# A chunked linear recurrence and a feed-forward layer on one core: static stages against a list-scheduled, token-major kernel

## The chip, the cores and the metric

The kernel runs on one core of a Trainium2 chip. The metric is device microseconds of one execution, on the slowest core, which here is the only one. A run is called slow when it lies more than 1.5% above the fastest run of the same kernel on the same chip. Only fast runs enter a ratio.

Engine names follow the profile. PE does matmuls, PEld its weight loads, DVE is the vector engine, ACT the scalar engine, POOL is GpSimd, and SP issues loads.

## The reference

Four batches of eight heads with 768 tokens of 48 values go through a recurrence with a decaying state. The eight heads of a token are then joined to 384 values, which go through 384 → 2048 → 384 with a leaky ReLU.

```python
state = zeros(B, H, D, D)
for t in range(S):                               # S = 768, D = 48
    cur = u * k[t] (outer) v[t]
    y[:, :, t] = r[t] @ (state + cur)
    state = w * state + k[t] (outer) v[t]        # w per head and channel
x = y.transpose(0, 2, 1, 3).reshape(B * S, H * D)      # 3072 x 384
h = x @ w_in                                     # 384 x 2048
out = max(0.01 * h, h) @ w_out                   # 2048 x 384
```

Both kernels cut the recurrence into chunks of 128 tokens, six a batch, so there are 24 stages. Inside a chunk it is a masked product of scores with v, plus the state times a decayed r.

## The kernel before

Each head is padded from 48 to 64 columns, so the 384 values of a token become 512 and fill four slabs of 128 rows. The first layer therefore costs four matmuls for each block of 128 hidden columns. Order is fixed by hand: a stage has four insertion points, and each takes a set number of feed-forward matmuls.

```python
NSLAB = 4
MOE_INSERT = [5, 5, 9, 9]          # feed-forward matmuls allowed at each point of a stage
# ...
# POOL, at the start: seven stages of r, k and v (cast to bf16), then all the weights
for n in range(NRAW):
    issue_input_stage(n)
for dst_ap, src_ap in win_chunks:  sem_w1.inc(g.dma_start(dst_ap, src_ap), 16)
for dst_ap, src_ap in wout_chunks: sem_w2.inc(g.dma_start(dst_ap, src_ap), 16)
# ...
# DVE, one stage: leaky ReLUs of the stage before, preparation of stage n + 4, state
for n in range(NSTAGE):
    for (T, fb) in lrelu_slot[n]:
        lrelu(T, fb)               # scalar_tensor_tensor 128x512: max(0.01 * h, h)
    prep_part1(n + 4)              # k*u, r*(k*u)
    state_update(n)                # waits for the stage's output matmuls
    prep_part2a(n + 4)             # reduce; r*qdec; v*s
    prep_part2b(n + 4)             # k*kdec; k*kbar
# ...
# ACT: first-layer eviction, the input of lrelu
sem_evac.inc(ACT.activation(h_sb[j % NHB][:, :], bank[:, :], AF.Copy))
# SP: one DMA transpose of 128x2048 a stage.  PE: scores, output and state products a stage
```

## Time and profile before

| | before |
|---|---|
| time, median | 276.89 us |
| PE / DVE / ACT / POOL busy | 70% / 67% / 42% / 43% |
| PE busy in the first 80 us | 24.0 us |
| PE busy from 80 to 200 us | 96.9 of 120 us |
| PE busy from 200 us to the end | 73.2 of 76.4 us |

The shares of the span hide three different stages, so the next view cuts the span. First come the page's rows in 40 slices of 6.9 us; a digit is the busy share in tenths, and PEclk is the granted PE clock in tenths.

```profile
PE 194.1 (70%) x1487; PEld 107.6 (39%) x1504; DVE 185.7 (67%) x323; ACT 115.6 (42%) x202; POOL 117.6 (43%) x150
...
PE   0002340126959249779896789997999999999995
...
DVE  5089991060997998789979899998881691186000
...
POOL 8999998064151834616564627741051100000000
PEclk9999999999997757999999999997999999999999
```

The same by windows. Columns after the stretch: its length, then busy us (and instructions) of PE, PEld, DVE, ACT and POOL, then the granted clock, the DMA share and GB/s.

```profile
0.00:80.00 80.00, 24.01 (x210) 14.91 (x212) 46.08 (x93) 21.95 (x35) 57.23 (x78) 1.00 1.83 136
80.00:120.00 40.00, 25.63 (x195) 13.23 (x199) 35.00 (x58) 17.59 (x31) 16.74 (x21) 0.79 1.21 102
120.00:160.00 40.00, 33.48 (x279) 18.08 (x280) 36.75 (x61) 20.28 (x38) 20.63 (x25) 1.00 1.25 116
160.00:200.00 40.00, 37.80 (x314) 21.05 (x316) 36.79 (x65) 22.19 (x40) 16.43 (x19) 0.96 0.91 111
200.00:240.00 40.00, 39.79 (x312) 22.18 (x314) 20.01 (x34) 20.22 (x38) 6.57 (x8) 1.00 0.21 56
240.00:276.40 36.40, 33.42 (x186) 18.11 (x185) 11.08 (x16) 13.33 (x24) 0.00 (x0) 1.00 0.14 50
```

PE is nearly idle at first, then shares the time with a DVE that is 87 to 92% busy, then runs alone.

The chain of waits (start us, length us, what) shows how the middle is tied together. This is one stage of it:

```profile
143.38 0.43 DVE tmp_st L387
...
143.83 0.69 DVE LS L391
...
144.56 0.69 DVE s_tok L346
...
145.60 1.11 DVE QVK L355
146.72 0.77 DVE QVK L363
147.49 0.77 DVE KB L369
148.26 0.61 DVE gT L404
...
148.95 0.60 ACT h_sb L476
...
149.61 0.61 PE ps_moe L535 x2
```

PE waits for an eviction (L476), the eviction for a leaky ReLU to free its buffer (L404), and the leaky ReLU stands in DVE's fixed order behind a whole stage's preparation. The DVE products beside POOL's mask are long: the view of the kdec product's line gives min/median/max in ns.

```profile
L363 DVE TENSOR_TENSOR QVK<-raw,kdec x24: 412/633/864, 16.3 to 205.7; 128x512 bf16<-128x512 bf16 x24
```

### The profile page before, as it was taken

The numbers are of one execution on the slowest core, as the hardware profiler recorded it, in microseconds if no ns is written. First come the engines' busy times: TensorE is split into PE (matmuls) and PEld (weight loads), VectorE is DVE, ScalarE is ACT, GpSimd is POOL, SyncE is SP. The second block draws the span as 40 slices with busy tenths as digits, with TensorE's granted clock in tenths as the row PEclk, the third lists the DMA queues.
The fourth block names the chain that finished last, engine by engine and source line by source line (L and its number), as shares of the span: only waits on it lengthen the run. The fifth ranks groups of instructions, "written<-read, shape, count | busy, mean of one in ns | idle before, by whom it ended". The sixth has DMA issues, their size and how long they took to land.

```text
span 276.4 us, 4070 instructions
## 1 busy us (share of the span) xinstructions
PE 194.1 (70%) x1487; PEld 107.6 (39%) x1504; DVE 185.7 (67%) x323; ACT 115.6 (42%) x202; POOL 117.6 (43%) x150
## 2 busy tenths in 40 slices
PE   0002340126959249779896789997999999999995
PEld 0001230113424134346552356543565446545663
DVE  5089991060997998789979899998881691186000
ACT  1451220013536224473464464565545772365121
POOL 8999998064151834616564627741051100000000
PEclk9999999999997757999999999997999999999999
DMA  3999999999993999849999749994235000200212
GB/s 29 96 129 171 157 105 181 170 151 149 143 152 69 127 70 147 52 80 121 139 160 175 41 82 171 144 157 78 45 90 134 1 2 30 85 2 0 85 59 85
DMA packets 132100, 28.09 MB, mean 102 GB/s; under 512 B 126528, under 2 KB 131648, under 8 KB 132080
## 3 DMA queue, kind: packets, MB, share of 16 engines
q0 software_dynamic: 78704, 10.53, 70.4%
q1 hardware_dynamic: 49920, 12.59, 30.8%
q10 hardware_dynamic: 3456, 4.72, 4.9%
q8 instruction: 12, 0.20, 0.3%
q14 instruction: 8, 0.07, 0.1%
HBM read 20.84 MB, written 4.72 MB: 92 GB/s over the span
## 4 chain that ended last, share of the span: by engine, by line
PE 49%; DVE 21%; POOL 14%; DMA 10%; issue 3%; ACT 2%; ACTq 0%; POOLq 0%
PE ps_moe L540 20%; PE ps_moe L535 20%; DMA raw<-in_v_dram 10%; POOL raw L279 7%; DVE gT L404 6%; DVE QVK L355 3%; DVE LS L391 2%; DVE s_tok L346 2%; DVE QVK L363 2%; POOL raw L275 2%; PE ps_ytr L595 2%; POOL w_out_sb L301 2%; DVE KB L369 2%; PE ps_at L555 2%; PE ps_sinc L576 2%
## 5 line engine op out<-in xcount | busy, mean ns | idle before, releaser
L535 PE MATMUL ps_moe<-xT,w_in_sb 128*128 128x512 bf16 x367 | 93.1, 399 | 16.9 <-ACT h_sb L476 14.0
L476 ACT ACTIVATE h_sb<-ps_moe 128x512 bf16<-128x512 f32 x96 | 57.0, 597 | 50.4 <-DVE gT L404 31.2
L404 DVE SCALAR_TENSOR_TENSOR gT<-h_sb 128x512 bf16<-128x512 bf16 x96 | 63.2, 711 | 14.2 <-ACT h_sb L476 14.0
L540 PE MATMUL ps_moe<-w_out_sb,gT 128*128 128x384 bf16 x384 | 66.6, 326 | 0.0
L535 PEld LDWEIGHTS ps_moe<-xT,w_in_sb 128*128 128x128 bf16 x384 | 37.0, 102 | 58.8 <-ACT h_sb L476 15.7
L463 ACT ACTIVATE ATf<-ps_at 128x512 bf16<-128x512 f32 x48 | 27.7, 596 | 60.8 <-PE ps_at L555 46.1
L279 POOL DMA_DIRECT2D raw<-in_r_dram x24 | 21.7, 906 | 72.5 <-PE ps_ytr L597 70.9
L288 POOL TENSOR_SCALAR_AFFINE_SELECT ATm<-ATf 128x512 bf16<-128x512 bf16 x44 | 34.6, 810 | 30.2 <-ACT ATf L463 30.2
L540 PEld LDWEIGHTS ps_moe<-w_out_sb,gT 128*128 128x128 bf16 x384 | 36.4, 98 | 23.2
L555 PE MATMUL ps_at<-TP 128*128 128x128 bf16 x96 | 11.0, 246 | 47.5 <-DMA TP<-QVK 46.5
L387 DVE TENSOR_TENSOR tmp_st<-LS,WLT 64x512 bf16<-64x512 bf16 x20 | 9.1, 454 | 30.2 <-PE ps_ytr L597 29.9
L555 PEld LDWEIGHTS ps_at<-TP 128*128 128x128 bf16 x96 | 6.4, 107 | 49.4 <-issue 24.0
L481 ACT ACTIVATE out_sb<-ps_moe 128x384 f32<-128x384 f32 x24 | 11.8, 492 | 32.7 <-PE ps_moe L540 32.4
L279 POOL DMA_DIRECT2D raw<-in_v_dram x24 | 21.8, 910 | 0.0
L279 POOL DMA_DIRECT2D raw<-in_k_dram x24 | 21.6, 900 | 0.0
L336 DVE TENSOR_TENSOR ku_buf<-raw,u_tab 128x512 bf16<-128x512 bf16 x24 | 11.4, 476 | 15.0 <-DMA raw<-in_v_dram 15.0
L355 DVE TENSOR_TENSOR QVK<-raw,s_tok 128x512 bf16<-128x512 bf16 x24 | 20.3, 845 | 0.0
L595 PE MATMUL ps_ytr<-ATm,raw 128*64 128x128 bf16 x192 | 16.1, 244 | 3.4 <-DVE ATm L377 2.0
L576 PE MATMUL ps_sinc<-raw,KB 128*64 128x64 bf16 x160 | 9.9, 212 | 11.6 <-DVE LS L391 11.6
L346 DVE TENSOR_REDUCE s_tok<-tmp_buf 128x8 f32<-128x512 bf16 x24 | 16.5, 686 | 0.8
L454 ACT ACTIVATE xT<-ps_ytr 128x512 bf16<-128x512 f32 x24 | 14.4, 600 | 4.9 <-PE ps_ytr L597 4.4
L595 PEld LDWEIGHTS ps_ytr<-ATm,raw 128*64 128x64 bf16 x192 | 11.3, 120 | 11.7 <-issue 9.0
(49 smaller groups left out, 159.7 us busy)
## 6 DMA issues: line engine op xcount, KB each, us to landing
out_dram<-out_sb ACTq DMA_DIRECT2D x24, 192.0 KB, 1.9
raw<-in_r_dram POOLq DMA_DIRECT2D x24, 96.0 KB, 5.2
raw<-in_k_dram POOLq DMA_DIRECT2D x24, 96.0 KB, 5.4
raw<-in_v_dram POOLq DMA_DIRECT2D x24, 96.0 KB, 6.2
w_in_sb<-in_moe_w_in_dram POOLq DMA_DIRECT2D x8, 192.0 KB, 11.8
w_out_sb<-in_moe_w_out_dram POOLq DMA_DIRECT2D x8, 192.0 KB, 18.5
TP<-QVK SPq DMA_TRANSPOSE x24, 5.6
lnw_bc<-in_w_dram POOLq DMA_DIRECT2D x1, 192.0 KB, 4.8
```

Of the source, the lines that this page charges most:

```text
L279: sem_in[bi].inc(g.dma_start(raw[bi][:, xi, :, 0:D], srcap), 16)
L288: inst = g.affine_select(ATm[pi][:, 4 * q:4 * q + 4, :], ATf[q][:, :, :], pattern=[[0, 4], [1, 128]], compare_op=ALU.is_ge, fill=0.0, base ...
L346: sc.inc(V.tensor_reduce(s_tok[pi][:, :], tmp_buf[pi][:, :, :], AX.X, ALU.add))
L355: iv = V.tensor_tensor(QVK[bi][:, :, 0:E], raw[ri][:, 2, :, :], s_tok[pi][:, :].unsqueeze(2).to_broadcast([128, H, E]), ALU.mult)
L404: inst = V.scalar_tensor_tensor(gT[T % 2][:, fb, :], h_sb[j % NHB][:, :], LRELU_SLOPE, h_sb[j % NHB][:, :], ALU.mult, ALU.max)
L463: sem_atev.inc(ACT.activation(ATf[q][:, :, :], ps_at[q][:, :].rearrange("p (m i) -> p m i", i=128), AF.Copy))
L476: sem_evac.inc(ACT.activation(h_sb[j % NHB][:, :], bank[:, :], AF.Copy))
L535: inst = PE.matmul(bank[:, :], w_in_sb[:, m, 128 * gd["x"]:128 * gd["x"] + 128], xT[:, m, 512 * gd["T"]:512 * gd["T"] + 512], start=first, ...
L540: inst = PE.matmul(bank[:, 0:DM], gT[gd["T"] % 2][:, s, 128 * gd["x"]:128 * gd["x"] + 128], w_out_sb[:, s, :], start=first, stop=lastm)
L555: last = PE.matmul(ps_at[0][:, 128 * hh:128 * hh + 128], TP[bi1][:, 2 * hh + 1, :], TP[bi1][:, 2 * hh, :])
L576: last = PE.matmul(ps_sinc[64:128, 64 * hh:64 * hh + 64], KB[bi1][:, hh, :], raw[ri1][:, 2, hh, :])
L595: PE.matmul(ps_ytr[pi][prow, pcol], raw[ri][:, 2, hh, :], ATm[pi][:, hh, :], start=True, stop=False)
```

## The change

The kernel is written anew. It builds a list of operations with estimated durations, reads, writes and buffer pools, and a list scheduler orders every engine's instructions and derives the semaphores. The intent is to keep PE full. The work itself changes too:

- x is dense (three slabs instead of four), because the recurrence's output is token-major and PE transposes it.
- The decay is centred, so that tables serve 256 tokens. The state stays in PSUM over two chunks.
- Loads go uncast from SP's queue. The u-bonus moves to POOL, and the score mask to DVE, read from PSUM.
- The first eight stages are transposed on PE, and later ones by DMA, at half the size.
- The leaky ReLU is an eviction, a scaled copy (by ACT or by DVE) and one wide maximum on DVE over 2048 columns.
- Feed-forward groups of one stage (the first two), then of two, are interleaved with the recurrence from the first stage on; the kernel before groups four stages. Filler matmuls are meant to keep PE's clock up at the start.

```diff
-NSLAB = 4
-MOE_INSERT = [5, 5, 9, 9]
+GROUPS = [1, 1] + [2] * 11
+TWO = [1, 1, 1, 1] + [1, 1, 0, 0] * 4 + [0, 0, 0, 0]
+QKT_DMA_FROM = 8
+WARM_UNTIL = 14.0
+DMA_SEQ = "st0 wc st1 u wi0@rk0 wi1@rk0 st2@v1 wo0@rk2 st3@v2 wo1@v2 st4@rk3"
 # ... the scheduler: among the ready operations of an engine the earliest start, then priority
+                    key = (max(st, free[e] + 0.02), o.prio)
+                    if best is None or key < best[0]:
+                        best = (key, o, st, sl)
 # ... loads: 0.14 and 0.07 us of SP time are planned, 2.1 and 1.05 us of transfer
+        o1 = op("SP", 0.14, go_rk, f"ldrk{n}", prio, writes=[vr], xfer=2.1, ndma=2, after=after)
+        o2 = op("SP", 0.07, go_v, f"ldv{n}", prio + 0.01, writes=[vrv], behind=[o1], xfer=1.05)
 # ... weights: 0.48 us of transfer are planned for a block of 128 hidden columns
+                  writes=[f_wi[i]], after=after, xfer=0.48 * WI[i], sem=f"wi{i}")
 # ... one stage of the recurrence
+        o = op("DVE", 0.96, lambda: V.tensor_tensor(kq.t[:, :, 0:D], ..., tab[l]..., ALU.mult), ...)
+            op(bn, bd_, lambda: be.tensor_tensor(pu.t[:, :, :], vr.t[:, 1, :, :], ubc[:, :, :], ALU.mult), ...)   # POOL
+            op(bn, bd_, lambda: be.tensor_tensor(pr.t[:, :, :], pu.t[:, :, :], vr.t[:, 0, :, :], ALU.mult), ...)  # POOL
+            op("DVE", 1.23, lambda: V.tensor_tensor(at.t[:, :, :], xy..., tri..., ALU.mult), ...)
+        op("DVE", 0.57, lambda: V.tensor_tensor(ys.t[:, :], y.t[:, 0:DM], bv.t[:, :], ALU.add), ...)
 # ... first layer of T stages: three slabs
+                    for s in range(3):
+                        o = PE.matmul(bk.t[:, 128 * T * f:128 * T * (f + 1)], win[:, s, 128 * fb:128 * fb + 128],
+                                      xT[:, s, L * n0:L * n0 + L * T], start=(s == 0), stop=(s == 2))
+            e1 = op("ACT", 0.52, (lambda ev=ev: ev(False)), f"ga_{n0}_{j}", ...)                 # eviction
+            if two:
+                hparts.append(op("ACT", 0.52, (lambda ev=ev: ev(True)), f"gb_{n0}_{j}", ...))     # times 0.01
+                m = op("DVE", 1.22 if nu == 4 else 0.69, ..., ALU.max)                            # 2048 wide
 # ... everything else cut
```

## The prediction

> **What bounds the kernel now.** No single engine: busy shares over the span are PE 70%, DVE 67%, ACT 42%, POOL 43% (page, part 1). (a) Until about 70 us the inputs bind: PE is busy 24.0 of the first 80 us (windows), and the longest piece of the chain of waits is 26.3 us for one v load queued behind the weights on POOL's queue. (b) From 80 to 200 us a static stage order binds: DVE is busy 108.5 of 120 us, PE only 96.9, and the chain alternates between DVE, one eviction, two matmuls. A stage takes 10.5 us; PE's clock falls to 0.79 over 80–120 us. (c) From 200 us PE is dense (39.8 of 40 us): 76 us of left-over feed-forward.
>
> **What changes, with costs.** In dense stretches of the chain 128x512 costs 219 ns (49 in 10.74 us), 128x384 costs 163 ns (128 in 20.81 us), attention matmuls of 128 columns 82 ns (4 in 0.33 us); half-array ones in alternating halves 28 ns.
> - PE: dense x drops the fourth slab: first layer from 384x219 = 84 us to 63. Second layer stays 62.6. Recurrence, estimated per stage: 8 half-row score matmuls 0.3, 12 output matmuls 0.7, state 0.27, transposes 0.24 = 1.5 us, plus 0.65 for the first 8 stages' PE transposes: about 41. Sum 167 us.
> - DVE: six 512-wide bf16 products a stage, the state multiply-add and 96 scalar_tensor_tensor (63 us) go. Come: one 768-wide product (0.9), the mask from PSUM (1.2), reduction, output add and state mask (0.5 each), wide max (1.2), half a scale (0.3): about 5.1 a stage, 125–140 us in all.
> - ACT: 96 first-layer evictions, 48 second ones for the scaled copy, three 384-wide copies a stage (492 ns): about 120 us busy.
> - POOL: mask and load issue go; three fp32 products a stage come, about 0.95 us each (estimate). SBUF — State Buffer, "Who interferes with whom", in the Trainium skill says a DVE operation with two SBUF inputs contends with GpSimd reads of SBUF; this trace agrees (the kdec product: 412 ns alone, about 850 beside the mask). I allow 0.5 us a stage.
> - DMA: loads move to SP, uncast; weights stay on POOL, but interleaved; stages from 8 transpose half as much as now.
>
> **Critical path.** The gain is packing: PE from 70% to about 86%. Start: first load lands near 5 us, table, scores, mask, output and transposition put the first feed-forward near 13 us; weights and five stages need about 30–35 us of DMA (this trace moved 120–190 GB/s of destination bytes), so some 16 us of PE's 167 are done by 34 us. The remaining 151 run near-dense, then about 4 us of last eviction and store: 189. I add 3–4% for waits: **195 us, 182 to 213**. Faster by over 2%: 0.97; within 2%: 0.015; slower: 0.015.
>
> **What would show it.** Right: PE over 85% busy in every slice from about 35 us to the end, granted clock 1.0, chain mostly first- and second-layer matmuls, DVE about 70–75%, ACT 60–65%, POOL under 45%, no 76 us tail. Step wrong if: PE under 60% before 45 us (weights late); PE idle on ACT evictions or DVE maxima in steady state; the scores or output matmuls cost twice my 1.0 us; waits for kt transposes after stage 8.
>
> **What would make it wrong.** Low DMA rate for 192-byte fp32 pieces beside the weights (to 215); DVE–POOL contention lifting DVE past 6.7 us a stage; lateness propagating through the fixed order. Lower if weights land by 25 us.

## More of the kernel before

The experiments were run on three chips, on which the kernel before had fast means of 273.4, 274.3 and 278.6 us, so absolute times are compared only within a chip.

In the first stretch the first feed-forward matmul starts only at 66.7 us, and PE's largest wait is for DMA transposes of the prepared operands. The view of waits gives, after the arrow, us in total, times and the longest:

```profile
PE ps_at L555 <- DMA TP<-QVK: 46.5, 4, 24.0
```

All four waits lie in the first 80 us; the longest runs from the start of the program to 24 us. A transpose took a median of 9.7 us from issue to landing in the first 80 us, and 4.9 us after that. (The clock of 1.00 that the windows give for the first 80 us does not fit the matmuls: sixteen output matmuls started 50 ns apart at 55 us and 28 ns apart at 75 us.)

## The result, and the profile after

The ratio is the mean time of one kernel's fast runs over that of the other's of the same rounds, so it is not quite the ratio of the medians quoted. It is 0.7238, with a 95% interval of 0.7177 to 0.7298.

| | before | after |
|---|---|---|
| time, median | 276.89 us | 199.80 us (198.27 to 200.67) |
| span of the profiled run | 276.4 us | 198.9 us |
| PE busy | 194.1 us | 175.0 us, of it 7.8 us filler |
| DVE busy | 185.7 us | 133.3 us |
| ACT busy | 115.6 us | 116.0 us |
| POOL busy | 117.6 us | 83.5 us |

Of the 77.5 us that the span lost, 19.1 us is less PE time, and the rest, 58.4 us, is idle PE time that went away (82.3 to 23.9 us). Most of it lies at the start: in the first 80 us PE was idle 56.0 us before and 19.1 us after, in the rest of the span 26.3 and 4.8 us. The page's rows after, in slices of 5.0 us:

```profile
PE 175.0 (88%) x1753; PEld 127.3 (64%) x1753; DVE 133.3 (67%) x179; ACT 116.0 (58%) x226; POOL 83.5 (42%) x82
...
PE   7640989488998998999998999999999999999983
...
DVE  2521605876999999899796784975975538364531
...
POOL 2310350435699999967867455541331100000000
PEclk9995557879999999999999999999999999999999
```

The windows after, with the same columns as before:

```profile
0.00:20.00 20.00, 8.83 (x82) 6.50 (x83) 6.21 (x21) 6.15 (x12) 3.53 (x13) 0.87 0.85 157
20.00:40.00 20.00, 15.82 (x181) 13.77 (x182) 10.41 (x17) 11.75 (x23) 6.72 (x8) 0.67 0.91 140
40.00:50.00 10.00, 8.49 (x79) 5.32 (x78) 6.86 (x10) 2.75 (x7) 4.66 (x5) 0.89 1.15 234
50.00:80.00 30.00, 27.71 (x300) 20.04 (x299) 29.69 (x35) 22.50 (x47) 27.70 (x23) 1.00 0.86 175
80.00:190.00 110.00, 108.69 (x1088) 78.80 (x1087) 77.67 (x97) 71.31 (x138) 40.88 (x36) 1.00 0.58 118
190.00:198.90 8.90, 5.45 (x33) 2.87 (x31) 2.48 (x3) 1.53 (x3) 0.00 (x0) 1.00 0.14 47
```

From 80 to 190 us PE is 99% busy: the long middle is now bound by matmuls, not by the chain through DVE. Two stretches are not. From 50 to 80 us DVE (29.69 of 30) and POOL (27.70) are both full, and PE loses 2.3 us. In the first 50 us PE is busy 33.1 us, 7.8 of them filler. The chain of waits at the start:

```profile
6.97 11.94 DMA raw<-in_k_dram
18.93 0.97 DVE kq L457
19.95 1.05 PE ps_g L484 x8
...
22.28 1.39 PE ps_g L636 x12
```

The second stage's k, issued at 6.97 us, landed near 18.9 us, because the first-layer weights (3.1 MB read from memory) were issued by POOL from 6.1 us (in a_weights_wait, below, with these weights held back, it landed at 10.5 us). DVE's fixed order has the second stage's product ahead of the first stage's output sum, which was ready at about 11 us and ran at 19.81 us. The first feed-forward matmul began at 22.2 us, at half clock: twelve 128-column matmuls took 1.39 us, where the same twelve took 0.67 us later. The Trainium skill, page "TensorE: Matmul & The Clock Gate", section "Part 1: The HAM clock gate", says that an idle PE falls back to half its clock. The trace agrees: PE ran no matmul between 12 and about 20 us, and the granted clock fell from 1.00 to 0.50 near 15 us. It stayed at 0.50 until 32 us in this run, although PE was busy 87% from 20 to 30 us. How long it stays there differs between runs of one and the same kernel. The first line is this run, the second a_control, the unchanged kernel on another chip (columns as above):

```profile
20.00:30.00 10.00, 8.71 (x90) 7.86 (x91) 3.48 (x7) 5.55 (x11) 4.42 (x5) 0.50 0.86 133
20.00:30.00 10.00, 8.55 (x122) 7.82 (x123) 4.50 (x10) 6.48 (x13) 4.42 (x5) 0.78 0.83 126
```

In a_control the first-layer matmuls were back at full pace by 26 us, and its span was 195.8 us instead of 198.9. How much of that difference the clock makes was not isolated, but the start of a single profile has to be read with it in mind.

In the DVE-bound stretch the operations take longer than alone. Three lines of the timeline (start us, length us, engine, instruction):

```profile
57.87 1.57 DVE L457 TENSOR_TENSOR kq<-raw,tab 128x768 bf16<-128x768 f32 x1
...
61.16 1.85 DVE L691 TENSOR_TENSOR gring<-gring,h 128x2048 bf16<-128x2048 bf16 x1
...
61.88 1.98 POOL L467 TENSOR_TENSOR pu<-raw,ubc 128x384 f32<-128x384 f32 x1
```

Their medians over the run are 0.95, 1.22 and 1.00 us. This is the contention that the prediction cited from "SBUF — State Buffer", and both sides pay it; a_pool_memset, below, puts it to the test.

### The profile page after: what moved, and what is told of

Read it like the earlier page. It is cut to its first block, busy times and chain, and to the rows that moved or that the text cites. A ratio compares the mean times of both kernels' runs of the same rounds, so it can differ in the third digit from the quotient of the medians.

```text
span 198.9 us, 4292 instructions
## 1 busy us (share of the span) xinstructions
PE 175.0 (88%) x1753; PEld 127.3 (64%) x1753; DVE 133.3 (67%) x179; ACT 116.0 (58%) x226; POOL 83.5 (42%) x82
## 4 chain that ended last, share of the span: by engine, by line
PE 58%; DVE 22%; ACT 7%; DMA 6%; SPq 3%; issue 2%; ACTq 0%; DVEq 0%
PE ps_g L711 26%; PE ps_g L636 22%; DVE gring L691 7%; DMA raw<-in_k_dram 6%; ACT gring L669 4%; DVE kq L457 4%; DVE at L552 3%; PE ps_xy L535 3%; DVE y L575 2%; PE ps_g L613 2%; PE ps_g L484 1%; PE ps_g L568 1%; ACT h L668 1%; PE ps_g L564 1%; DVE h L687 1%
## 5 line engine op out<-in xcount | busy, mean ns | idle before, releaser
L636 PE MATMUL ps_g<-xT,win 128*128 128x256 bf16 (+1 forms) x624 | 75.9, 274 | 1.3 <-ACT xT L616 1.3
L711 PE MATMUL ps_g<-wout,gring 128*128 128x384 bf16 x384 | 68.5, 331 | 3.5 <-DVE gring L691 3.2
L669 ACT ACTIVATE gring<-ps_g 128x512 bf16<-128x512 f32 x96 | 57.8, 606 | 21.9 <-PE ps_g L636 15.4
L636 PEld LDWEIGHTS ps_g<-xT,win 128*128 128x128 bf16 x624 | 56.8, 103 | 9.1 <-ACT xT L616 2.1
L711 PEld LDWEIGHTS ps_g<-wout,gring 128*128 128x128 bf16 x384 | 36.4, 99 | 28.6 <-DVE gring L691 5.6
L691 DVE TENSOR_TENSOR gring<-gring,h 128x2048 bf16<-128x2048 bf16 (+1 forms) x26 | 32.5, 1253 | 11.0 <-ACT h L668 9.4
L552 DVE TENSOR_TENSOR at<-ps_xy,tri 128x1024 bf16<-128x1024 f32 x22 | 26.8, 1217 | 15.6 <-PE ps_xy L535 15.6
L457 DVE TENSOR_TENSOR kq<-raw,tab 128x768 bf16<-128x768 f32 x24 | 27.0, 1127 | 12.3 <-DMA raw<-in_k_dram 7.9
L668 ACT ACTIVATE h<-ps_g 128x512 bf16<-128x512 f32 x48 | 28.6, 614 | 1.1 <-PE ps_g L636 0.9
L469 POOL TENSOR_TENSOR pr<-pu,raw 128x384 f32<-128x384 f32 x22 | 27.2, 1235 | 1.3
L471 DVE TENSOR_REDUCE b<-pr 128x8 f32<-128x384 f32 x22 | 11.9, 541 | 2.6 <-POOL pr L469 1.4
```

The lines of the kernel that those rows point to most:

```text
L457: o = op("DVE", 0.96, lambda: V.tensor_tensor(kq.t[:, :, 0:D], vr.t[:, 0:2, :, :].rearrange("p a h d -> p (a h) d"), tab[l][:, :, :, :].re ...
L469: op(bn, bd_, lambda: be.tensor_tensor(pr.t[:, :, :], pu.t[:, :, :], vr.t[:, 0, :, :], ALU.mult), f"pr{n}", pr_a(n, 0.3), reads=[vr, pu], ...
L552: op("DVE", 1.23, lambda: V.tensor_tensor(at.t[:, :, :], xy.t[:, :].rearrange("p (h t) -> p h t", t=128), tri[:, :].unsqueeze(1).to_broadc ...
L636: o = PE.matmul(bk.t[:, 128 * T * f:128 * T * (f + 1)], win[:, s, 128 * fb:128 * fb + 128], xT[:, s, L * n0:L * n0 + L * T], start=(s == 0 ...
L668: return A.activation(o_ap, i_ap, AF.Copy, scale=LRELU_SLOPE)
L669: return A.activation(o_ap, i_ap, AF.Copy)
```

## The experiments

Names beginning with a_ change the kernel after, names beginning with b_ the kernel before. Each ratio is to the kernel before on the same chip.

### Undo the interleaving (a_serial)

```diff
-               reads=[xtv[n] for n in range(n0, n0 + T)] + wchunks, writes=[bk])
+               reads=[xtv[n] for n in range(n0, n0 + T)] + wchunks, writes=[bk],
+               after=list(xtv[NST - 1].writers))
```

> The kernel after, with the interleaving undone: every first-layer group waits for the last stage's recurrence. It measures the two halves by themselves. Theory: the recurrence alone is bound by inputs and DVE at about 4 to 5 us a stage, so ends at 110 to 135 us; the feed-forward alone is 126 us of matmuls, 135 to 145 with evictions; together 245 to 275 us, which gives back most of the 77 us gained. Rival: the gain is mostly the smaller work and the faster start; then 215 to 235 us.

Measured: 281.97 us, ratio 1.032 (1.021 to 1.043), correct. That is a little slower than the kernel before and above the range that the theory gave. The two halves by windows:

```profile
0.00:137.60 137.60, 70.42 (x749) 48.90 (x749) 91.84 (x139) 28.64 (x60) 78.51 (x82) 0.56 0.89 160
137.60:279.80 142.20, 130.87 (x1008) 95.61 (x1008) 39.17 (x40) 89.26 (x167) 0.00 (x0) 0.98 0.10 34
```

The recurrence alone takes 137.6 us, in which DVE is busy 67% and POOL 57%, with PE at a granted clock of 0.56. No one engine is full there, and what bounds it was not tested. The feed-forward alone takes 142.2 us. Interleaved they take 198.9 us, so 81 us of the 280 are hidden by overlap. That is about as much as the whole gain. It does not follow that the interleaving made the whole gain, because the kernel before interleaves as well, by its four insertion points; how much its own overlap is worth was not measured. What is shown is that the rest of the rewrite, with no interleaving at all, is no faster than the kernel before with its own. The recurrence by itself also ran at half clock almost throughout, so part of its length is that.

### Put the fourth slab back (a_slab4)

```diff
-                    for s in range(3):
+                    for s in range(4):
-                        o = PE.matmul(..., win[:, s, 128 * fb:128 * fb + 128], xT[:, s, ...], start=(s == 0), stop=(s == 2))
+                        o = PE.matmul(..., win[:, s, 128 * fb:128 * fb + 128] if s < 3 else zer[:, 0:128],
+                                      xT[:, min(s, 2), ...], start=(s == 0), stop=(s == 3))
 # cut: the planned duration of a piece rises from 0.65 to 0.87 us; the pieces wait for the zero weights
```

> The kernel after, with a fourth, zero-weight 128-row matmul added to every first-layer sum, so that dense x is undone in time only; the result stays right. Theory: from about 35 us on PE bounds, so the whole cost shows: 384 x 256-column-equivalents are 24 x 16 x 128 columns, 21 us at full clock: 217 to 222 us. Rival: DVE and its lock with POOL set the pace between 50 and 80 us (DVE 98% busy there), so part of it hides: 208 to 215 us.

Measured: 216.83 us (fast runs 214.78 and 215.61), ratio 0.787 (0.776 to 0.798), correct. Against the ratio of the change itself, 0.724, this is about 17 us more (0.063 times 273.4 us). It lies below the theory's range in the fast runs and just above the rival's. About four fifths of the 21 us show, so PE bounds most of the kernel but not all of it. The profile, taken on a slow run, shows where part may have hid: from 20 to 80 us PE was busy 53.1 us, against 51.1 us in the unchanged kernel (a_control), time in which PE would otherwise have waited.

### Dense x alone, in the kernel before (b_3slab)

```diff
-                groups.append(dict(kind="g1", T=T, x=fb, nmm=NSLAB, s_idx=len(groups)))
+                groups.append(dict(kind="g1", T=T, x=fb, nmm=3, s_idx=len(groups)))
```

> The kernel before, with only three of the four 128-row slabs summed in the first layer: the cost of dense x alone, without its layout; the result is wrong on purpose. Theory: up to 200 us the kernel before is not bound by PE, so the 21 us of matmuls saved show only where PE is dense (the last 76 us and pieces of 120 to 200 us): 8 to 14 us gained, ratio 0.95 to 0.97. Rival: PE binds on the whole: 18 to 21 us gained, ratio 0.925 to 0.935.

Measured: 267.04 us, ratio 0.958 (0.949 to 0.967). The result is wrong, on purpose. The fast runs gain 11.9 us (278.6 to 266.8), in the theory's range. The same matmuls are worth about 17 us in the kernel after and 12 in the kernel before: a saving on PE counts for more where PE binds more of the time.

### A larger allowance in the kernel before (b_budget)

```diff
-MOE_INSERT = [5, 5, 9, 9]
+MOE_INSERT = [8, 8, 12, 12]
```

> The kernel before, with 40 instead of 28 feed-forward matmuls allowed a stage (the feed-forward has 32 a stage). Theory: a stage of 80 to 200 us is set by the chain of DVE preparation, leaky ReLU and eviction (DVE busy 108.5 of 120 us), not by the allowance, so the tail shrinks by what the stages lengthen: within 2%. Rival: the allowance alone left the 76 us tail: 10 to 25 us gained (ratio 0.91 to 0.96).

Measured: 291.30 us, ratio 1.038 (1.023 to 1.053), correct. Both miss: it is slower. DVE's busy time from 120 to 160 us fell from 36.75 to 29.04 us, and DVE's state update waited 44.6 us for the stage's output matmuls instead of 29.9 (before first, then this run):

```profile
DVE tmp_st L387 <- PE ps_ytr L597: 29.9, 11, 13.6
DVE tmp_st L387 <- PE ps_ytr L597: 44.6, 13, 10.9
```

The longer pieces of feed-forward stand in PE's fixed order ahead of the recurrence that DVE waits for. The 76 us tail was thus not a matter of the allowance alone.

### Weights earlier in the kernel before (b_weights_early)

```diff
-            for n in range(NRAW):
+            for n in range(3):
                 issue_input_stage(n)
             g.wait_ge(sem_dvi.sem, 7)
             # ... the weights
+            for n in range(3, NRAW):
+                issue_input_stage(n)
```

> The kernel before, with the weights issued after three stages' loads instead of seven. Theory: the first 70 us, in which PE was busy 24 us, were lost to the order of the loads; feed-forward can start about 15 us earlier, and 5 to 15 us are gained (ratio 0.95 to 0.98). Rival: bytes and the static order bind: within 1%.

Measured: 283.32 us, ratio 1.017 (1.010 to 1.024), correct. Both miss again. The chain of waits names the reason:

```profile
38.08 12.43 DMA raw<-in_v_dram
...
50.54 0.43 DVE ku_buf L337
```

DVE prepares four stages before it masks the first one's scores. The fourth stage's load now stood behind the weights and landed at 50.5 us, and the first mask waited for it: it ran at 54.2 us instead of 31.3 (ACT stood 31.8 us at that point). The first feed-forward matmul came at 73.1 us instead of 66.7. Moving a load earlier moved a load that the fixed order needs first to a later place.

### The leaky ReLU inside the eviction (b_prelu and a_prelu)

In the kernel before:

```diff
-                    sem_evac.inc(ACT.activation(h_sb[j % NHB][:, :], bank[:, :], AF.Copy))
+                    sem_evac.inc(ACT.activation(gT[gd["T"] % 2][:, gd["x"], :], bank[:, :], AF.Prelu, alpha=LRELU_SLOPE))
 # DVE's lrelu calls are dropped; PE waits for the last eviction of its group
```

> The kernel before, with the leaky ReLU done in the eviction by the scalar engine's parametric ReLU, so that DVE's 96 scalar_tensor_tensor (63 us) go. Theory: DVE and the chain through it bind from 80 to 200 us, so a stage shortens from 10.5 to about 8 us there: 15 to 35 us gained (ratio 0.87 to 0.95), though the same edit brought the kernel after only 4.7 us. Rival: PE's fixed order and its tail bind, whatever DVE does: less than 8 us (ratio over 0.97).

Measured: 255.14 us, ratio 0.916 (0.908 to 0.924), correct. The windows answer to those of the kernel before:

```profile
80.00:120.00 40.00, 34.44 (x287) 18.56 (x290) 29.68 (x51) 22.12 (x39) 22.45 (x27) 0.87 1.79 130
120.00:160.00 40.00, 39.68 (x349) 22.64 (x351) 32.84 (x54) 23.24 (x42) 25.10 (x31) 1.00 1.50 149
160.00:200.00 40.00, 39.68 (x341) 21.85 (x343) 17.14 (x34) 25.86 (x47) 10.38 (x16) 1.00 0.53 93
```

PE rose from 33.48 to 39.68 us between 120 and 160 us. The reading of the kernel before holds: DVE, and the chain of buffers through it, bound that stretch. The start did not change: PE still waited 45.6 us for DMA transposes.

In the kernel after:

```diff
-                return A.activation(o_ap, i_ap, AF.Copy)
+                return A.activation(o_ap, i_ap, AF.Prelu, alpha=LRELU_SLOPE)
-            two = TWO[n0]
+            two = 0
 # no scaled copies, no wide maxima; the second layer waits for the evictions
```

> The kernel after, with the leaky ReLU done in the one eviction from PSUM by the scalar engine's parametric ReLU; the scaled copies, the wide scales and the wide maxima (41 us of DVE, 29 us of ACT) go. Whether the result is right is open. Theory: PE bounds from 80 us on, and DVE only between 50 and 80 us, where PE lost about 2.3 us, so with a third of DVE's work gone the gain is just 2 to 6 us (193 to 198). Rival: DVE and its contention with POOL are the real bound: 10 us or more (190 or less).

Measured: 194.49 us against 199.19 us for the unchanged kernel on the same chip, correct. The fast runs have means of 192.9 and 198.7 us, so 5.7 us are gained. The ratios are 0.704 (0.692 to 0.716) and 0.725 (0.717 to 0.732), so the intervals just miss each other. This version beats both kernels. Its profile (a run that counts as slow, at 195.28 us) shows the DVE-bound stretch gone:

```profile
50.00:80.00 30.00, 29.99 (x333) 22.30 (x332) 23.45 (x32) 17.36 (x34) 23.92 (x23) 1.00 1.01 194
80.00:190.00 110.00, 109.95 (x1096) 80.86 (x1093) 50.05 (x68) 59.92 (x114) 35.91 (x35) 1.00 0.56 117
```

DVE is busy 93.7 us instead of 133, and still only 5.7 us are gained, where the same edit gave the kernel before 23.5 us. With PE at 99% in the long middle there is little left for the others to give.

### Contention between DVE and POOL (a_pool_memset)

```diff
-            op(bn, bd_, lambda: be.tensor_tensor(pu.t[:, :, :], vr.t[:, 1, :, :], ubc[:, :, :], ALU.mult),
+            op(bn, bd_, lambda: be.memset(pu.t[:, :, :], 0.0),
-            op(bn, bd_, lambda: be.tensor_tensor(pr.t[:, :, :], pu.t[:, :, :], vr.t[:, 0, :, :], ALU.mult),
+            op(bn, bd_, lambda: be.memset(pr.t[:, :, :], 0.0),
```

> The kernel after, with the two POOL products of the bonus replaced by POOL memsets that read nothing, in the same planned order; the result is wrong on purpose. Theory: contention between DVE and POOL lengthens DVE's wide maximum (1.33 us mean, 1.22 alone) and the kq product (1.13 mean, 0.95 alone), about 7 us of DVE in all, but PE bounds nearly everywhere, so only 1 to 3 us come back (197 to 199). Rival: the contention is a main loss of the middle: 5 us or more come back (195 or less).

Measured: 195.78 us, ratio 0.714 (0.706 to 0.722); the result is wrong, on purpose. The unchanged kernel's ratio on another chip is 0.725 (0.717 to 0.732), so some 3 us are suggested, between the two expectations, and the intervals overlap. (a_st1_early, which keeps the time of the kernel after, ran on the same chip: its mean is 3.3 us above that of these fast runs.) The kq product fell from a mean of 1127 ns to 972 ns, and the wide maximum from 1326 to 1278 ns, beside the POOL product that was left. This run also makes POOL faster (a memset takes 0.42 us, a product 1.0 alone), so it is an upper bound for the contention.

### The start (a_st1_early, a_weights_wait, a_weights_wait_warm, with a_control)

> The kernel after, unchanged, so that the next three have it on the same chip. Both theories: 198 to 201 us.

Measured: 199.19 us (197.60 to 201.09), ratio 0.725 (0.717 to 0.732).

First, the second stage's loads ahead of the small tables:

```diff
-DMA_SEQ = "st0 wc st1 u wi0@rk0 wi1@rk0 st2@v1 wo0@rk2 st3@v2 wo1@v2 st4@rk3"
+DMA_SEQ = "st0 st1 wc u wi0@rk0 wi1@rk0 st2@v1 wo0@rk2 st3@v2 wo1@v2 st4@rk3"
```

> The kernel after, with one edit: the second stage's loads are issued before the four tiny table loads of w and u, so that they go out ahead of the weights. Theory: between 11 and 19 us all engines stood still because DVE's fixed order put the second stage's product (whose load, issued at 6.5 us behind the weights, landed at 18.9) ahead of the first stage's output sum. With the load out early, that product should start at 9 to 11 us instead of 18.9 and the first feed-forward matmul at about 14 instead of 22.2; the rest of the weights still land near 18 to 20 us, so the gain is 3 to 6 us (194 to 197). Rival: the start is bound by the bytes of weights and inputs, in whatever order; then within 1.5 us of the kernel after.

Measured: 198.52 us, ratio 0.726 (0.720 to 0.732), correct. It is the kernel after, within the noise. The product did start at 10.00 us, but then a table took the load's place in the chain:

```profile
9.45 9.57 DMA ucol<-in_u_dram
```

A load of 0.8 KB took 9.57 us beside the weights, and the first feed-forward matmul came at 24.5 us.

Then the weights behind everything small:

```diff
-DMA_SEQ = "st0 wc st1 u wi0@rk0 wi1@rk0 st2@v1 ..."
+DMA_SEQ = "st0 wc st1 u wi0@v1 wi1@v1 st2@v1 ..."
```

> The kernel after, with one edit: the first-layer weights and the third stage's inputs start only when the second stage's v load has landed. Loading the second stage ahead of the tables moved the standstill instead of ending it: then a tiny u table, also behind the weights, held DVE's fixed order until 19.0 us. Theory: whatever small load shares the DMA engines with the 2 MB of first-layer weights lands when they do, and the fixed order stops there; with every small load ahead of the weights, the second stage's product starts at 9 to 13 us and PE has done both first stages' recurrence by 17 us, while the weights land near 22 us. The start is then bound by the weights, so 1 to 4 us are gained (195 to 198). Rival: the bytes alone count and the weights now start 5 us later, so it is 2 to 5 us slower.

Measured: 199.90 us, ratio 0.728 (0.724 to 0.733), correct. (The 2 MB of the expectation are 3.1 MB read and 1.5 MB written.) The first feed-forward matmul now began at 18.7 us instead of 22.4 (a_control), yet nothing was gained: the first second-layer matmul began at 38.0 us instead of 34.5. Part of that difference is the clock: from 20 to 35 us it was 0.50 in this profile and 0.85 in a_control's. Against the profile of the change (0.60, 36.6 us) it is 1.4 us. The chain now runs through the third stage's v load, which took 14.81 us beside the weights.

Then the same with measured durations in the plan and filler to 24 us:

```diff
-WARM_UNTIL = 14.0
+WARM_UNTIL = 24.0
-        o1 = op("SP", 0.14, go_rk, ...          xfer=0.48 * WI[i] ... xfer=0.48 * WO[i]
+        o1 = op("SP", 1.0, go_rk, ...           xfer=0.7 * WI[i] ...  xfer=0.7 * WO[i]
 # ldv 0.07 -> 0.9, the two table loads 0.14 -> 1.15 and 0.9
```

> As the last, and the scheduler is given transfer and issue times nearer to those measured (0.7 us instead of 0.48 for each 128-column weight block, 0.9 to 1.15 us instead of 0.07 to 0.14 for load issues), and its filler matmuls run to 24 us of the plan. Theory: PE's granted clock, 0.50 between 20 and 30 us in the kernel after, stays at 1.0 when the first-layer matmuls start, and the plan's order fits what happens: another 3 to 5 us less than the last (191 to 195). Rival: the clock of this stretch does not matter, since the second-layer weights (landing near 38 us) bind it: within 1.5 us of the last.

Measured: 203.14 us, ratio 0.741 (0.737 to 0.746), correct: slower, which neither side expected. The clock from 20 to 30 us was 0.74 instead of 0.50, but a_control, without the longer filler, had 0.78, so this does not show that the filler did it. PE lost 1.9 us more between 80 and 120 us than in the run before (37.22 against 39.07 us busy), and the end came later. Two things were changed at once, so the plan's new order and the filler cannot be told apart here.

Together these runs say that the order of the small loads was not what the start costs. The prologue's idle time from 11 to 19 us is real and can be moved, but nothing is gained after it. In the six profiles looked at (the four of this section, the profile of the change, and a_prelu) the second layer began between 34.5 and 39.0 us. It did not wait for its own weights in the profile after: the first half of them landed at 31.8 us, and its first matmul, at 36.6 us, stood in PE's order behind output matmuls that waited for DVE's mask. What the six share is the end of the loading: in every order the weights and the first four stages were in only by 37 to 40 us, with DMA kept busy (share 0.91 to 1.15, as the windows count it, from 20 to 50 us in the profile after). That fits a limit by bytes, but no run removed bytes, and the clock, which differed between the profiles, was not held fixed. What sets the length of the start stays open.

## Why the prediction was right

The estimate was 195 us with a range of 182 to 213 us; 199.8 us was measured. Point by point:

**What bound the kernel before.** The middle as a chain through DVE is shown by b_prelu, which takes DVE's leaky ReLU away and gains 23.5 us, and by b_budget, which asks PE for more and loses. The first stretch was put down to inputs behind the order of loads. That is not what b_weights_early shows: moving the weights made it slower, through DVE's fixed order. What is shown is that the load order and the order on DVE cannot be judged apart. Why the first 70 us of the old kernel cost what they do stays open. The prediction names the loads only; the record also has the 46.5 us in which PE waited for DMA transposes, and feed-forward in groups of four stages, which began at 66.7 us. The kernel after changed both, and no run tested either alone.

**The gain is packing.** Right: PE's share went from 70 to 88% (86% predicted), and a_serial shows the overlap to be worth 81 us in the kernel after. The 81 us are not added to the other savings; they need each other. Without the interleaving the whole rewrite is 3% slower than the kernel before, which interleaves too. Of the 58.4 us of idle PE time that went away, 36.8 us lie in the first 80 us. Which of the changes there (PE transposes, smaller groups, loads on another queue, the scheduler's order) brought them was not separated.

**The sum.** The prediction had 167 us of dense PE work, 16 of it done by 34 us, the rest near-dense, then 6 us of waits and 4 of tail. Three terms were mis-sized, and it is luck that they partly cancel. The following estimates count matmuls in the trace at the durations of its dense pieces.

| term | predicted | measured or worked out from the trace after |
|---|---|---|
| first layer | 63 us | 63.4 us (0.66 us for six of 256 columns, 0.67 for twelve of 128) |
| second layer | 62.6 us | 62.6 us (2.61 us for sixteen) |
| recurrence | 41 us | about 35 us, an estimate (a stage: scores 0.33, outputs 0.25 + 0.20, state 0.28, transposes 0.27; 0.45 for the transposes of each of the first 8 stages; some of these pieces took 0.17 us where they were densest, which would give about 29) |
| done by 34 us | 16 us | 9.4 us |
| done by 50 us | 32 us (16, then dense) | 19 us |
| lost after 50 us | 10 us | 7 us (2.3 to 80 us, 1.3 to 190 us, 3.5 in the tail) |

At 50 us it was 13 us behind the prediction. It had 6 us less to do, and it lost 3 us less later; 13 − 6 − 3 = 4 us, which is the difference of 198.9 and 195 us.

**The start is the term that was off.** The prediction had "the first feed-forward near 13 us"; it was 22.2 us, and 24.5 and 18.7 us in two variants. It also took the weights and five stages to be in by 30 to 35 us with PE working meanwhile. The first layer's second block of weights alone landed near 18.5 us, the last block of the second layer's near 38.6 us, the second layer began at 36.6 us, and until then PE had dense work only in part, at half clock for some of it. The prediction's own sign of late weights, PE under 60% before 45 us, was seen: without the filler PE was busy 21.1 of the first 45 us.

**DVE under PE.** The prediction allowed 0.5 us a stage for contention and expected PE over 85% busy in every slice from 35 us. PE was busy 44% from 35 to 40 us, which belongs to the start, and fell just below 85% in a few later slices (82% from 60 to 65 us). From 50 to 80 us DVE was 99% busy. The mechanism was named correctly, and its price was small: 2.3 us of PE time in that stretch, and 5.7 us for all of DVE's leaky-ReLU work (a_prelu).

**What was seen as predicted.** DVE busy 133 us (125 to 140), ACT 116 (120), POOL 42% (under 45%), no tail of left-over feed-forward, and a chain made mostly of first- and second-layer matmuls (26% and 22% of the span). The granted clock of 1.0, predicted from 35 us, held only from 50 us on.

## What to carry to other kernels

Where two kinds of work bind different engines, overlapping them can be worth more than the savings of work: here 280 us one after the other, 199 us interleaved. Before crediting or planning a saving, ask what binds in the stretch where it falls: the same edit (the ReLU in the eviction) gave 23.5 us where DVE was in the chain and 5.7 us where PE was full, and the same matmuls saved were worth 12 us in one kernel and 17 in the other. With a fixed order on each engine a late input stops everything planned behind it, so a change of load order has to be judged together with the order on the engine that waits; three changes at the start of the kernel after gained nothing (medians of 198.5, 199.9 and 203.1 us against 199.2). And one profile is not the kernel: in two profiles of the same kernel the half clock of the start ended near 25 us in one and near 32 us in the other.

## What the Trainium skill lacked or had wrong

- "ScalarE: Activation LUTs", the step "Same chain, other wiring": it describes the wiring of Parametric ReLU and says that none of it is reachable from a kernel today. Here the parametric ReLU with alpha 0.01 gave a correct result in both kernels. A 128x512 eviction took 597 ns against 606 for the plain copy in the kernel after, with no table load beyond the one at the start, and 596 against 597 in the kernel before. How the engine computes it, the runs do not show.
- "TensorE: Matmul & The Clock Gate", section "Back-to-back issue gap": it gives sustained gaps of about 81 ns for 128 columns and 131 ns for 512, with a weight load for each matmul. In the kernel before 512 columns took 219 ns (49 in 10.74 us), and in the kernel after 128 columns took 56 ns (12 in 0.67 us), in both with a weight load for each. These are near the gaps that the section gives for an isolated matmul, about 216 and 56 ns. The 82 ns that the prediction takes for 128 columns (4 in 0.33 us) include the delay before the first of the four; the rest started 55 to 67 ns apart.
- The same page, "Part 1: The HAM clock gate", does not say how busy a PE may be and still be held at half clock. In a_serial the granted clock was 0.50 from 20 to 140 us, while PE was 40 to 62% busy in each 20 us of it; in the profile after it was 0.50 from 20 to 30 us with PE 87% busy.
- "DMA: Bandwidth & Descriptors" has no figure for a tiny load beside large ones. Here a load of 0.8 KB took 9.57 us to land beside the weights, against a median of 1.9 us in the kernel after, where it went out just ahead of them.
